# Weights of a mixer stage turned from 64-bit to 32-bit numbers: leading part plus the rest, with an accumulating transfer for the channel weights

## The chip, the cores and the metric

The kernel runs on one NeuronCore of one Trainium2 chip. The metric is the device time of one execution in microseconds (us). The kernel before takes 478.04 us, the median of 3 runs (477.49 to 479.05).

The engines that matter are TensorE (PE in the profile; its weight loads are listed apart as PEld), VectorE (DVE), ScalarE (ACT), GpSimd (POOL) and SyncE (SP), which here only issues transfers. An engine takes its own instructions strictly in the order in which they stand in its program and waits on semaphores for the others.

## The reference

Two stages follow each other for each of 4 batches. The first is a linear attention with a decaying state (8 heads of 48, 768 tokens):

```python
for t in range(S):
    cur = einsum('bhd,bhe->bhde', u[None] * kt, vt)
    y[:, :, t] = einsum('bhd,bhde->bhe', rt, state + cur)
    state = wt[:, :, :, None] * state + einsum('bhd,bhe->bhde', kt, vt)
```

Its output, as x of 768 tokens by 384 channels per batch, goes through a mixer over tokens and then one over channels:

```python
h  = maximum(x.T @ w_tok1, 0) @ w_tok2        # 768 -> 256 -> 768, over tokens
u  = x + h.T
h2 = maximum(u @ w_ch1, 0) @ w_ch2            # 384 -> 1536 -> 384, over channels
out = u + h2
```

The four weights are made as float32 numbers times a numpy scalar of 64 bits, and come to the kernel as 64-bit floating point. [...]

## The kernel before, in words

**Attention.** Each batch is cut into 3 units of 256 tokens. For one unit, DVE runs two scans over the decays (`ends` L456, `begins` L464) and scales keys and queries (L461, L467). PE makes the products inside chunks of 64 tokens (`grams` L336), the state updates (`outer` L386, `update` L529) and the outputs (`across` L401, `within` L422). ACT scales the state from chunk to chunk (`scaled` L522), copies the results out of PSUM (`taken` L428), and reads the range of the decays into flags (`ranges` L448). In batch 0 the state goes around a ring: ACT scales it (L522), PE adds the next chunk to it (L529), ACT scales the sum, twelve chunks long.

**Mixer.** In batch 0, PE runs `hidden` (L968), `back` (L979), a transposition (`turn` L990), `up` (L1014) and `down` (L1025) with float32 weights; ACT rectifies (L971, L1017) and copies the transposed rows (L992), DVE adds into x (L981). From batch 1 on, PE uses split forms of the weights, which ACT and DVE make from the converted ones (`splits`, L600 to L622).

**Conversion.** `conversion` cuts the weights into steps of 128 partitions by 1024 numbers: 3 steps for the two token weights, 9 for the two channel weights (steps 0 to 8 here; w_ch1 fills steps 0 to 3 and half of step 4, w_ch2 the rest). Before, a step is two loads of 512 KB (L280), then: DVE masks the exponent out of the top 16 bits (`exponent` L283) and the mantissa out of the high word (`mantissa` L289) and adds the low word times 2^-32 to it (`add` L295); ACT makes a power of two from the exponent (`raise_two` L286) and a sign from the high word (`signs` L292); DVE multiplies the two (`signed` L298), and multiplies the mantissa by that (`put` L305, in two instructions where a step spans two weights or a piece doesn't lie in one pattern).

**What sets the order.** The list in the call of `strict` at L1116 to L1131 fixes the order of every engine up to the first `back`, by hand. It holds the three steps of the token weights and step 0 of the channel weights. From there on, the digits of `ORDER` say which of nine streams gives the next piece, and `weights_in_turn` (L1196) is the stream of the channel steps, each laid out by `single` (L1137). In `single` the tuples with a queue and a duration are costs for the planner that once made `ORDER`; they set no time when the kernel runs. Each engine keeps that order exactly. Loads of a step go out on SP's queue, two steps ahead, and wait until the raw words of the step that used the room before are read. POOL has no work of the conversion; its first product (L786) comes far behind it.

**Who needs a step.** PE's `up` for the hidden blocks 0 to 3 needs steps 0 and 1, blocks 4 to 7 steps 1 and 2, blocks 8 to 11 steps 3 and 4. PE does `up` for two segments of 256 tokens in turn: the first four matmuls of block 0 need step 0 alone, the fifth needs step 1. `down` follows, in pairs of blocks, twice each, over steps 4 to 8.

Of the kernel before, what the change touches and what calls it, by code (L numbers as in the profile page):

```python
# [10 lines left out]
f32 = mybir.dt.float32  # L11
# [4 lines left out]
u16 = mybir.dt.uint16  # L16
u32 = mybir.dt.uint32
# [47 lines left out]
def rwkv6_then_mixer(  # L65
# [8 lines left out]
    w_tok1: bass.AP,  # L74
    w_tok2: bass.AP,
    w_ch1: bass.AP,
    w_ch2: bass.AP,
# [157 lines left out]
    wtok2 = wts.tile([128, DTOK // 128, S], f32, name="wtok2")  # L235
    now = {"wch1": wts.tile([128, DM // 128, DCH], f32, name="wch1"), "wch2": wts.tile([128, NJ, DM], f32, name="wch2"),
           "wtok1": wtok1, "wtok2": wtok2}

    def conversion_tiles(name):
        t = wide.tile([128, 12 * PIECE], u32, name=name, tag="raw")  # L240
        return t[:, :7 * PIECE], t[:, ds(7 * PIECE, 4 * PIECE)], t[:, ds(11 * PIECE, PIECE)]

    scratch, spare, powers = conversion_tiles("raw")
# [3 lines left out]
    def conversion_rooms(scratch, spare, powers):  # L247
        return ([t[:, :4 * PIECE] for t in (scratch, spare, early[0])], [scratch[:, ts(2, 2 * PIECE)], early[1][:, :2 * PIECE]],
                [[t.bitcast(u16) for t in (scratch[:, ts(6, PIECE)], powers)], [early[1][:, ts(n, PIECE)].bitcast(u16) for n in (2, 3, 4)]])

    bits64, mantissas, exponents = conversion_rooms(scratch, spare, powers)

    def convert(pair, raw, room, signs_at=None):

        d64 = bits64[raw]
        lo, hi = (d64.rearrange("p (n two) -> p n two", two=2)[:, :, j] for j in range(2))
        top = d64.bitcast(u16).rearrange("p (n four) -> p n four", four=4)[:, :, 3]
        m, planes = mantissas[room], exponents[room]
        mf, e, power = m.bitcast(f32), *planes[:2]
        sign, factor = planes[2 * room].bitcast(bf16) if signs_at is None else signs_at, power.bitcast(bf16)  # L260

        (a, _), (b, _) = pair
        c, k = a.shape[1:]
        (row, _), (one, _) = a.ap[1:]
        apart = b.offset - a.offset if a.tensor is b.tensor else None
        beside = apart == k * one
        if beside:
            whole = bass.AP(a.tensor, a.offset, [list(a.ap[0]), [row, c], [one, 2 * k]])
        elif apart is not None and (c == 1 or apart == c * row):
            whole = bass.AP(a.tensor, a.offset, [list(a.ap[0]), [apart // c, 2 * c], [one, k]])  # L270
        else:
            whole = None

        def load():
            for n, (dst, src) in enumerate(pair):
                if beside:
                    to = d64.rearrange("p (c n k) -> p n c k", n=2, c=c)[:, n]
                else:
                    to = d64[:, ts(n, 2 * PIECE)].rearrange("p (c k) -> p c k", c=dst.shape[1])
                sp.dma_start(to, src)  # L280

        def exponent():
            dve.tensor_scalar(e, top, 0x7FF0, None, op0=ALU.bitwise_and)  # L283

        def raise_two():
            act.activation(power, e, AF.Relu, bias=rebias, scale=8.0)  # L286

        def mantissa():
            dve.tensor_scalar(m, hi, 0xFFFFF, 0x100000, op0=ALU.bitwise_and, op1=ALU.bitwise_or)  # L289

        def signs():
            act.activation(sign, hi.bitcast(i32), AF.Sign)  # L292

        def add():
            dve.scalar_tensor_tensor(mf, lo, 2.0 ** -32, m, op0=ALU.mult, op1=ALU.add)  # L295

        def signed(on=dve):
            on.tensor_tensor(factor, factor, sign, ALU.mult)  # L298

        def put(whole_step=True):  # L300
            if whole_step:
                signed()
            for dst, cols in [(whole, slice(0, 2 * PIECE))] if whole is not None else [(dst, ts(n, PIECE)) for n, (dst, _) in enumerate(pair)]:
                x, by = (t[:, cols].rearrange("p (c k) -> p c k", c=dst.shape[1]) for t in (mf, factor))
                dve.scalar_tensor_tensor(dst, x, 2.0 ** -20, by, op0=ALU.mult, op1=ALU.mult)  # L305

        put.apart = lambda on: (lambda: signed(on), lambda: put(False))
        return load, exponent, mantissa, raise_two, add, signs, put

    def blocks(t, src, c, k):  # L310

        bits = src.bitcast(u32).rearrange("(c p) k -> p c k", p=128)
        at = [(i, j) for j in range(0, t.shape[2], k) for i in range(0, t.shape[1], c)]
        return [(t[:, ds(i, c), ds(j, k)], bits[:, ds(i, c), ds(2 * j, 2 * k)]) for i, j in (sorted(at) if c == 4 else at)]

    def conversion(*weights, rooms):
        pieces = [e for w in weights for e in blocks(*w)]
        return [convert(pieces[2 * n:2 * n + 2], *rooms(n)) for n in range(len(pieces) // 2)]
# [992 lines left out]
    with within_range.Else():  # L1311
# [8 lines left out]
        for steps in conversion((now["wtok1"], w_tok1, 2, 256), (now["wtok2"], w_tok2, 2, 256), rooms=lambda n: (n % 2, n % 2)):  # L1320
            for f in steps:
                f()
# [39 lines left out]
```

## Time and profile before

| What | us |
|---|---|
| median of 3 runs | 478.04 (477.49 to 479.05) |
| profiled execution, first to last instruction (span) | 476.6 |
| busy time of PE, PEld, DVE, ACT, POOL in it | 458.4, 409.1, 353.0, 263.8, 54.2 |

The profile has no separate time for the execution that it shows; the median of the runs is 1.4 us above its span, which holds what lies around the first and last instruction and the difference between executions. The profile's page lists busy time by engine, then the span in 40 slices, then the chain of work that ended last, followed back from the end: an engine with a large share there sets the time. Further views of the same trace are used: groups of instructions of one shape, the busy time of each engine in stretches of the span, instructions in order of time with the idle time before them and its releaser in square brackets, the chain in order of time (start, duration, what), and the issues of transfers with their time to landing. PE lists a float32 matmul of `up` as two records.

### The profile page before, as it was taken

The page shows a single profiled execution, that of the slowest core. Times are in us where ns is not written, and L with a number is a line of the kernel's source. Part 1 is how long each engine was busy: PE and PEld are TensorE (multiplying, and loading weights), DVE is VectorE, ACT ScalarE, POOL GpSimd, SP SyncE. Part 2 cuts the span into 40 slices and gives each one's busy share as a digit, 9 for nine tenths or more (in the row PEclk, how much of TensorE's full clock was granted, in tenths as well). Part 3 has the DMA queues.
Part 4 walks back from the last instruction along what each step waited for, and adds up shares of the span by engine and source line. Part 5 has one row for each costly group of instructions (what it writes and reads, how often), then busy time and mean ns, then how long its engine had stood idle before and what let it go on. Part 6 is the DMA issues. An engine that isn't in the chain of part 4 may idle for free.

```text
span 476.6 us, 12802 instructions
## 1 busy us (share of the span) xinstructions
PE 458.4 (96%) x5322; PEld 409.1 (86%) x5322; DVE 353.0 (74%) x506; ACT 263.8 (55%) x606; POOL 54.2 (11%) x58
## 2 busy tenths in 40 slices
PE   3799999999999999999999999999999999999995
PEld 2686688856797668999999999999999999999995
DVE  7999899998598877876897998685587885235331
ACT  6689876773678856353747485251827554134040
POOL 1000000000000001140303002130304003022030
PEclk9979999999999999999999999999999999999999
DMA  8956946753585556853979752754785503437321
GB/s 304 335 170 217 253 146 193 235 221 99 147 232 136 179 189 219 267 182 99 272 275 237 278 158 55 211 168 143 205 230 162 176 30 91 124 86 211 86 86 54
DMA packets 49984, 85.35 MB, mean 179 GB/s; under 512 B 4928, under 2 KB 40640, under 8 KB 49920
## 3 DMA queue, kind: packets, MB, share of 16 engines
q1 hardware_dynamic: 49632, 84.37, 56.9%
q8 instruction: 43, 0.70, 0.6%
q14 instruction: 21, 0.17, 0.1%
q10 hardware_dynamic: 288, 0.10, 0.1%
HBM read 72.65 MB, written 11.80 MB: 177 GB/s over the span
## 4 chain that ended last, share of the span: by engine, by line
PE 92%; DMA 3%; ACT 2%; DVE 1%; SPq 1%; issue 0%; DVEq 0%; ACTq 0%
PE bank L1025 10%; PE bank L793 8%; PE bank L800 8%; PE bank L795 8%; PE bank L811 8%; PE bank L813 8%; PE bank L812 8%; PE bank L1014 7%; PE bank L688 3%; PE bank L747 3%; PE bank L1010 3%; PE bank L336 2%; PE bank L422 2%; PE bank L401 2%; PE kv_ps L386 2%; PE bank L690 2%
## 5 line engine op out<-in xcount | busy, mean ns | idle before, releaser
L786 POOL TENSOR_TENSOR z_high<-z_high 128x384 fp32r<-128x384 f32 x48 | 52.9, 1107 | 406.0 <-DMA ring<-third 186.3
L775 ACT ACTIVATE z_high<-bank 128x384 fp32r<-128x384 f32 x48 | 23.5, 489 | 57.8 <-PE bank L800 57.3
L793 PE MATMUL bank<-x_forms,forms 128*128 128x384 f32 x216 | 50.3, 341 | 0.0
L800 PE MATMUL bank<-z_more,forms 128*128 128x384 f32 x216 | 50.1, 340 | 0.0
L782 DVE SCALAR_TENSOR_TENSOR z_high<-bank,z_high 128x384 fp32r<-128x384 f32 x48 | 26.5, 555 | 30.9 <-ACT z_high L775 30.1
L795 PE MATMUL bank<-x_forms,ring 128*128 128x384 f32 x216 | 49.3, 337 | 0.0
L1025 PE MATMUL bank<-wch,z 128*128 128x384 f32 x144 | 48.1, 488 | 0.0
L811 PE MATMUL bank<-forms,z_high 128*128 128x384 f32 x140 | 47.8, 341 | 0.0
L819 DVE SCALAR_TENSOR_TENSOR x<-bank,x 128x384 f32<-128x384 f32 x35 | 18.8, 553 | 39.0 <-PE bank L813 38.9
L813 PE MATMUL bank<-forms,z_high 128*128 128x384 f32 x140 | 47.1, 337 | 0.0
L812 PE MATMUL bank<-ring,z_high 128*128 128x384 f32 x140 | 47.1, 337 | 0.0
L1025 PEld LDWEIGHTS bank<-wch,z 128*128 128x128 f32 x144 | 26.8, 190 | 17.2
L522 ACT ACTIVATE before<-state,to_end 112x48 f32<-112x48 f32 x132 | 33.2, 324 | 11.8 <-DVE state L537 7.6
L800 PEld LDWEIGHTS bank<-z_more,forms 128*128 128x128 f32 x216 | 39.0, 188 | 0.1
L793 PEld LDWEIGHTS bank<-x_forms,forms 128*128 128x128 f32 x216 | 38.3, 188 | 0.5
L795 PEld LDWEIGHTS bank<-x_forms,ring 128*128 128x128 f32 x216 | 38.6, 188 | 0.0
L1014 PE MATMUL bank<-xT,wch 128*128 128x256 f32 x144 | 32.0, 381 | 0.0
L1014 PEld LDWEIGHTS bank<-xT,wch 128*128 128x128 f32 x144 | 27.0, 190 | 3.7
L778 ACT ACTIVATE z_high<-z_high 128x384 fp32r<-128x384 f32 x48 | 25.2, 525 | 3.6
L811 PEld LDWEIGHTS bank<-forms,z_high 128*128 128x128 f32 x140 | 26.3, 188 | 0.2
L812 PEld LDWEIGHTS bank<-ring,z_high 128*128 128x128 f32 x140 | 26.3, 188 | 0.0
L813 PEld LDWEIGHTS bank<-forms,z_high 128*128 128x128 f32 x140 | 26.3, 188 | 0.0
(252 smaller groups left out, 969.2 us busy)
## 6 DMA issues: line engine op xcount, KB each, us to landing
ring<-third SPq DMA_DIRECT2D x144, 192.0 KB, 3.2
raw<-in_w_ch_dram SPq DMA_DIRECT2D x16, 512.0 KB, 4.8
rk<-in_rk_dram SPq DMA_DIRECT2D x36, 192.0 KB, 5.5
near<-in_near_dram SPq DMA_DIRECT2D x8, 768.0 KB, 6.0
w<-in_w_dram SPq DMA_DIRECT2D x10, 520.5 KB, 5.1
vt<-in_v_dram SPq DMA_DIRECT2D x12, 384.0 KB, 5.1
out_dram<-x SPq DMA_DIRECT2D x17, 192.0 KB, 2.5
third<-forms SPq DMA_DIRECT2D x12, 192.0 KB, 4.0
```

What stands on the lines that cost most here:

```text
L522: act.mul(t[:ROWS, a], state[bt, g][:ROWS, a], by_last(c, j)[:, a:a + 1])
L778: act.mul(z_form(jt, 2), z_form(jt, 0).bitcast(f32), 1.0 / BASE)
L782: dve.scalar_tensor_tensor(z_form(jt, 1), a, 0.0, z_form(jt, 0).bitcast(f32), op0=ALU.max, op1=ALU.subtract)
L786: pool.tensor_add(z_form(jt, 2), z_form(jt, 2).bitcast(f32), z_form(jt, 1).bitcast(f32))
L793: pe.matmul(a, up[m], xf(0)[:, m], start=m == 0, stop=False)
L795: pe.matmul(a, low[:, m], xf(1)[:, m], start=False, stop=False)
L800: pe.matmul(banks["a", jt], joint, xf(2)[:, m], start=False, stop=m == 2)
L811: pe.matmul(a, z[0], up, start=first, stop=False, skip_group_check=True)
L812: pe.matmul(a, z[1], held[bt, s, half, 1, jt], start=False, stop=False, skip_group_check=True)
L813: pe.matmul(a, z[2], joint, start=False, stop=last, skip_group_check=True)
L1014: pe.matmul(ps, now["wch1"][:, m, ts(jt, 128)], xT[:, m, ts(s, SEG)], start=(m == 0), stop=(m == DM // 128 - 1))
L1025: pe.matmul(ps, zs[s][:, jt, ts(n, 128)], now["wch2"][:, jt, :], start=(jt == 0), stop=(jt == NJ - 1))
```

## The change

A step's 64-bit number is now taken as a leading part and a rest. The load leaves out the lowest 16 bits, so that the words in SBUF are shifted: the top 16 bits (sign, exponent, 4 bits of mantissa) are one 16-bit integer, and the next 32 bits are one 32-bit word. Eight times the top 16 bits, with the bias moved, are the bits of a bf16 number. ACT writes that for positive numbers (`positive`) and for negative ones (`negative`), both by a rectified linear function, DVE subtracts the two (`lead`), and the result is the leading part with its sign. DVE masks the mantissa away to get the signed power (`raise_two`), multiplies the rest by 2^-36 and the power into the weight's place (`put`), and the leading part is added last. For the token weights DVE does that (`add`); for the channel weights GpSimd issues a transfer from SBUF to SBUF that accumulates in the destination (`add_landing`: bf16 in, added to float32, 1024 numbers on each of 128 partitions; 10 transfers, as step 4 needs two).

The host lays the words out so that a step is one load of 4095 16-bit units on each of 128 partitions in place of two loads with shorter rows. The token weight `wtok2` and the channel weight `wch1` change their layout in SBUF with it, and PE reads them there. PE's order is unchanged.

```diff
+        word = raw_words[raw]
+        rest = word.rearrange("p (n two) -> p n two", two=2)[:, :, 0]
+        top = word.bitcast(i16).rearrange("p (n four) -> p n four", four=4)[:, :, 2]
+        plus, minus = parts[room]
+        leading, power = plus.bitcast(bf16), minus.bitcast(bf16)
         def load():
...
-                sp.dma_start(to, src)
-        def exponent():
-            dve.tensor_scalar(e, top, 0x7FF0, None, op0=ALU.bitwise_and)
-        def raise_two():
-            act.activation(power, e, AF.Relu, bias=rebias, scale=8.0)
-        def mantissa():
-            dve.tensor_scalar(m, hi, 0xFFFFF, 0x100000, op0=ALU.bitwise_and, op1=ALU.bitwise_or)
-        def signs():
-            act.activation(sign, hi.bitcast(i32), AF.Sign)
+            sp.dma_start(word.bitcast(u16)[:, :words.shape[1]], words)
+        def positive():
+            act.activation(plus, top, AF.Relu, bias=rebias, scale=8.0)
+        def negative():
+            act.activation(minus, top, AF.Relu, bias=rebias, scale=-8.0)
+        def lead():
+            dve.tensor_sub(plus, plus, minus)
+        def raise_two():
+            dve.tensor_scalar(minus.bitcast(u16), plus.bitcast(u16), 0xFF80, None, op0=ALU.bitwise_and)
+        def put():
+            for dst, cols in to:
+                dve.scalar_tensor_tensor(dst, rest[:, cols], 2.0 ** -36, power[:, cols], op0=ALU.mult, op1=ALU.mult)
         def add():
-            dve.scalar_tensor_tensor(mf, lo, 2.0 ** -32, m, op0=ALU.mult, op1=ALU.add)
-        def signed(on=dve):
-            on.tensor_tensor(factor, factor, sign, ALU.mult)
-        def put(whole_step=True):
...
-                dve.scalar_tensor_tensor(dst, x, 2.0 ** -20, by, op0=ALU.mult, op1=ALU.mult)
+            for dst, cols in to:
+                dve.tensor_add(dst, dst, leading[:, cols])
+        def add_landing():
+            for dst, cols in to:
+                pool.dma_start(out=dst, in_=leading[:, cols], accum_op=ALU.add)
...
+            steps.append(convert(to, words.bitcast(u16)[n, :, 1:], *rooms(n)))
...
+    for name, of in (("words_tok", (rows("w_tok1"), grouped(rows("w_tok2"), 256))), ("words_ch", (grouped(rows("w_ch1"), PIECE), rows("w_ch2")))):
...
-        whole = [("load", load, ("Q", 5.0, last(2, "add", "signs"))), ("signs", signs, ("ACT", 1.15, k("load") + last(2, "put"))),
-                 ("exponent", exponent, ("DVE", 0.69, k("load") + last(1, "two"))), ("two", raise_two, ("ACT", 1.15, k("exponent") + last(1, "put"))),
-                 ("mantissa", mantissa, ("DVE", 0.69, k("load") + last(1, "put"))), ("add", add, ("DVE", 1.23, k("mantissa"))),
-                 ("put", put, ("DVE", 2.06, k("two", "add", "signs")))]
+        whole = [("load", load, ("Q", 5.0, last(2, "value", "minus"))), ("plus", positive, ("ACT", 1.15, k("load") + last(2, "put"))),
+                 ("minus", negative, ("ACT", 1.15, k("load") + last(2, "value"))), ("lead", lead, ("DVE", 0.69, k("plus", "minus"))),
+                 ("two", raise_two, ("DVE", 0.35, k("lead"))), ("value", put, ("DVE", 1.23, k("two"))), ("put", add, ("Q", 4.0, k("value")))]
```

`ORDER` is unchanged. A channel step still has seven pieces, so a digit of the stream of weights now stands for another piece than before; the list in the call of `strict` is written out anew for the token steps and step 0. Three places matter below. In the rows that follow, line numbers of the kernel before are 17 to 28 above those of the changed one.

On ACT, around the end of `hidden` (the h rows are the rectified sums), the kernel before has

```order
L292 ACTIVATE raw<-xT 128x1024
L292 ACTIVATE z_130<-z_129 128x1024
L971 ACTIVATE h_145<-h_ps 128x384 x2
L286 ACTIVATE z_130<-z_130,rebias 128x1024
L448 ACTIVATE junk,flags<-first,most 112x1041
L448 ACTIVATE junk,flags<-to_end_93,most 112x1041
L292 ACTIVATE first<-raw 128x1024
L286 ACTIVATE raw<-raw,rebias 128x1024
```

and the changed kernel has

```order
L264 ACTIVATE z_130<-z_129,rebias 128x1024
L267 ACTIVATE z_130<-z_129,rebias 128x1024
L954 ACTIVATE h_145<-h_ps 128x384 x2
L431 ACTIVATE junk,flags<-to_end_93,least 112x1041
L431 ACTIVATE junk,flags<-first,most 112x1041
L431 ACTIVATE junk,flags<-to_end_93,most 112x1041
L264 ACTIVATE raw<-raw,rebias 128x1024
L267 ACTIVATE raw<-raw,rebias 128x1024
```

The last two rows of each are step 1 of the channel weights. Between h and them stand one step of the conversion and two readings of ranges before, and three readings of ranges now; the third one stood further ahead.

On DVE, the same place (the x rows are `back`'s sums). Before:

```order
L298 TENSOR_TENSOR z_130<-z_130 128x1024
L305 SCALAR_TENSOR_TENSOR wch_126<-z_130 128x2x512
L283 TENSOR_SCALAR raw<-raw 128x1024
L981 TENSOR_TENSOR x<-x,bank_881 128x384
L981 TENSOR_TENSOR x<-x,bank_882 128x384
L289 TENSOR_SCALAR raw<-raw 128x1024
L295 SCALAR_TENSOR_TENSOR raw<-raw 128x1024
L981 TENSOR_TENSOR x<-x,bank_884 128x384
L298 TENSOR_TENSOR raw<-raw,first 128x1024
L305 SCALAR_TENSOR_TENSOR wch_126<-raw 128x2x512
```

and now:

```order
L277 SCALAR_TENSOR_TENSOR wch_126<-z_129,z_130 128x1024
L964 TENSOR_TENSOR x<-x,kv_ps 128x384
L964 TENSOR_TENSOR x<-x,bank_873 128x384
L964 TENSOR_TENSOR x<-x,bank_874 128x384
L270 TENSOR_TENSOR raw<-raw 128x1024
L273 TENSOR_SCALAR raw<-raw 128x1024
L277 SCALAR_TENSOR_TENSOR wch_126<-raw 128x1024
L964 TENSOR_TENSOR x<-x,bank_876 128x384
```

Step 0 ends on DVE ahead of `back`'s sums now, and step 1 (`lead`, `raise_two`, `put`) is three rows in place of five. Behind each L277 row, GpSimd issues the accumulating transfer of that step.

On ACT again, further on, among the rectified blocks of `up` (z rows), with what each row waits for, where steps 6, 7 and 8 of the channel weights stand. Before:

```order
L286 ACTIVATE raw<-raw,rebias 128x1024 [waits DVE_49]
L1017 ACTIVATE z_129<-bank_886 128x256 [waits PE_49]
L292 ACTIVATE first<-raw 128x1024 [waits DMAHW6_49,DMAHW5_49,Activation_49]
L1017 ACTIVATE z_130<-bank_881 128x256 [waits PE_49]
L1017 ACTIVATE z_129<-bank_884 128x256 [waits PE_49]
L286 ACTIVATE raw<-raw,rebias 128x1024 [waits DVE_49]
L448 ACTIVATE junk,flags<-to_end_93,most 112x1041 [waits Activation_49]
L292 ACTIVATE first<-raw 128x1024 [waits DMAHW7_49,DMAHW0_49,Activation_49]
```

and now:

```order
L267 ACTIVATE raw<-raw,rebias 128x1024
L1000 ACTIVATE z_130<-bank_874 128x256 [waits PE_49]
L1000 ACTIVATE z_129<-bank_878 128x256 [waits PE_49]
L264 ACTIVATE raw<-raw,rebias 128x1024 [waits DMAHW3_49,DMASW6_49,DVE_49]
L1000 ACTIVATE z_130<-bank_873 128x256 [waits PE_49]
L1000 ACTIVATE z_129<-bank_876 128x256 [waits PE_49]
L267 ACTIVATE raw<-raw,rebias 128x1024 [waits DVE_49]
L431 ACTIVATE junk,flags<-to_end_93,most 112x1041 [waits Activation_49]
L264 ACTIVATE raw<-raw,rebias 128x1024 [waits DMAHW4_49,DMASW7_49,DVE_49]
```

The first row of each is the second ACT instruction of step 6; now it stands one rectified block earlier than before. The last row is the first ACT instruction of step 8. Now it is `positive`, which writes the plane from which step 6's accumulating transfer reads, and so it waits for that transfer (DMASW7). In the same way the first split (L583), which writes into the room of the planes, now waits for the transfers of steps 7 and 8, where it waited for DVE.

143 lines of the change are left out of this document (61 added, 82 removed).

## The prediction

> **What bounds the kernel now.** I read the page first, for the engines and the chain that ended last.
>
> ```profile
> span 476.6 us, 12802 instructions
> PE 458.4 (96%) x5322; PEld 409.1 (86%) x5322; DVE 353.0 (74%) x506; ACT 263.8 (55%) x606; POOL 54.2 (11%) x58
> ...
> PE 92%; DMA 3%; ACT 2%; DVE 1%; SPq 1%; issue 0%; DVEq 0%; ACTq 0%
> ```
>
> PE is busy for 96% of the span and makes up 92% of the chain; DVE, which the change relieves, makes up 1%. Then the stretches of the span (from:to, length, busy time of PE, PEld, DVE, ACT, POOL, granted clock, share of the transfer engines, GB/s), to see where PE has holes:
>
> ```profile
> 12.00:24.00 12.00, 8.93 (x254) 7.26 (x254) 11.79 (x11) 7.44 (x22) 0.00 (x0) 0.91 0.93 331
> ...
> 36.00:48.00 12.00, 11.87 (x281) 7.93 (x280) 11.30 (x14) 11.07 (x27) 0.00 (x0) 1.00 0.62 220
> ...
> 60.00:72.00 12.00, 12.00 (x62) 10.61 (x61) 11.79 (x15) 8.78 (x18) 0.00 (x0) 1.00 0.40 131
> ...
> 84.00:96.00 12.00, 12.00 (x173) 9.87 (x172) 11.80 (x16) 8.51 (x14) 0.00 (x0) 1.00 0.84 254
> ```
>
> The holes are in the start. From 60 to 96 us DVE is nearly as full as PE, but PE has no hole there that a lighter DVE could close. The chain in order of time (start, duration, what) shows what stands on the path:
>
> ```profile
> 14.32 6.32 DMA first<-in_rk_dram
> ...
> 44.70 4.88 PE h_ps L968 x14
> ...
> 58.84 11.66 PE bank L1014 x54
> ...
> 73.67 17.03 PE bank L1014 x78
> ...
> 94.00 15.48 PE bank L1025 x48
> ```
>
> From 44.70 on PE runs through `hidden`, `back`, `up` and `down` back to back. A microsecond that PE waits here is one at the end; one that DVE saves here is worth nothing unless PE had waited for it.
>
> **What the change takes away and adds, by engine.** The groups of the first 135 us by shape (count, busy, mean ns of one, idle before):
>
> ```profile
> L295 DVE SCALAR_TENSOR_TENSOR raw<-raw 128x1024 f32<-128x1024 uint32 x9 | 11.0, 1223 | 0.2
> L305 DVE SCALAR_TENSOR_TENSOR wch<-raw 128x1024 f32<-128x1024 f32 x6 | 7.3, 1225 | 0.2
> ...
> L289 DVE TENSOR_SCALAR raw<-raw 128x1024 uint32<-128x1024 uint32 x9 | 6.2, 686 | 0.0
> L283 DVE TENSOR_SCALAR raw<-raw 128x1024 uint16<-128x1024 uint16 x9 | 6.1, 677 | 0.0
> ...
> L298 DVE TENSOR_TENSOR raw<-raw,first 128x1024 bf16<-128x1024 bf16 x8 | 5.5, 685 | 0.1
> ```
>
> A step cost DVE 0.68 + 0.69 + 1.22 + 0.69 + 1.23 = 4.5 us. Now `lead` is nearest to L298 (two 16-bit planes, 0.69) and `put` to L295 (1.22). The mask over a dense 16-bit plane has no row; L283 reads every fourth and takes 0.68, so it lies between 0 and 0.68, and I take 0.4. That is 2.3 us for a channel step and 3.5 with the token steps' `add` (1.22 more). DVE is spared 9 x 2.2 + 3 x 1.0 = 23 us, and none of it is on the path. ACT has two instructions of 1.15 us per step as before:
>
> ```profile
> L286 ACT ACTIVATE raw<-raw,rebias 128x1024 uint16<-128x1024 uint16 x10 | 11.5, 1148 | 6.0 <-DVE raw L283 5.9
> L292 ACT ACTIVATE first<-raw 128x1024 bf16<-128x1024 int32 x8 | 9.3, 1157 | 0.3 <-ACT junk L448 0.3
> ```
>
> The 5.9 us in which ACT waited for `exponent` go; what is late next behind them is PE's bank, as ACT's z rows wait for PE.
>
> **The start, up to 44 us.** PE goes step by step with ACT around the state's ring, and ACT has as many instructions in it as before, at the same places. ACT itself stands still once:
>
> ```profile
> 20.75 0.91 ACT L352 ACTIVATE near<-first,u_col 112x256 f32<-112x256 f32 x2 [3.12 <-DMA first<-in_rk_dram]
> ```
>
> That load is queued behind the raw words of the first token step, which now come in one transfer of longer rows that start 2 bytes off. The issue of a second load goes (SP), its bytes stay. No row has such a transfer; a gain of 0.3 or a loss of as much is my estimate from the 6.32 us that the row of the chain gives for the pair of loads, and I take 0. On DVE the token steps' rows move, so the masks must be looked at; the last one, of unit 2, is the tightest:
>
> ```profile
> 37.20 1.16 ACT L286 ACTIVATE z<-z,rebias 128x1024 uint16<-128x1024 uint16 x1
> ...
> 40.93 1.32 DVE L348 COPY_PREDICATED at<-before_it,gram 128x1024 f32<-128x1024 uint8 x1 [0.16 <-PE gram L336]
> ...
> 43.55 1.15 PE L422 MATMUL y_ps<-vt,at 64*64 64x48 f32 x64
> ```
>
> Token step 1's second part takes the place of the ACT row and ends at 38.3; `lead`, the mask of bits, and `put` and `add` in halves (0.6 + 0.4 + 2.4) end at 41.7, and the mask at 43.1, 0.45 ahead of the PE row that needs it. So the start stays.
>
> **The first term: step 1, at 60 us.** PE enters `up` at 58.84. The first four matmuls (8 records at 17.03 / 78 = 0.218 us) need step 0, so step 1 is needed at 60.6. Before, it was ready at 59.25 (last row):
>
> ```profile
> 49.61 0.49 ACT L971 ACTIVATE h<-h_ps 128x384 f32<-128x384 f32 x1 [0.80 <-PE h_ps L968]
> 50.00 1.14 ACT L286 ACTIVATE z<-z,rebias 128x1024 uint16<-128x1024 uint16 x1
> 51.04 1.15 ACT L448 ACTIVATE junk<-first,most 112x1041 uint8<-112x1041 f32 x1
> ...
> 53.48 1.14 ACT L292 ACTIVATE first<-raw 128x1024 bf16<-128x1024 int32 x1
> 54.52 1.14 ACT L286 ACTIVATE raw<-raw,rebias 128x1024 uint16<-128x1024 uint16 x1
> ...
> 58.02 1.23 DVE L305 SCALAR_TENSOR_TENSOR wch<-raw 128x1024 f32<-128x1024 f32 x1
> ```
>
> Now ACT reads three ranges after h, each (53.48 - 51.04) / 2 = 1.22, from 50.00 to 53.7, then makes step 1's two parts, 1.04 each from start to start, to 55.7. DVE follows with 0.7 + 0.4 + 1.22, to 58.1. There the conversion ended before; now an accumulating transfer begins. With X for the time from the end of `put` to the landing, PE waits 58.1 + X - 60.6 = **X - 2.5**.
>
> **X has no row.** GpSimd issues no transfer before. The nearest are SP's (bytes each, median us from issue to landing):
>
> ```profile
> raw<-in_w_ch_dram SPq DMA_DIRECT2D x16, 512.0 KB, 4.8
> ...
> near<-in_near_dram SPq DMA_DIRECT2D x8, 768.0 KB, 6.0
> ...
> out_dram<-x SPq DMA_DIRECT2D x17, 192.0 KB, 2.5
> ...
> z_more<-kept SPq DMA_DIRECT2D x2, 384.0 KB, 7.7
> ```
>
> A step's transfer writes 512 KB and reads 256 of the leading part and 512 of the destination, 768 in all. By what it writes it is nearest to the first row, by what it reads to the second; I take the middle, X = 5.4. Ends: 2.5 (192 KB, an idle queue) and 7.7 (384 KB among others). So the first term is 2.9, from 0 to 5.2.
>
> The Trainium skill ("DMA: Bandwidth & Descriptors", section "Anatomy of one DMA — SWDGE (gpsimd) path") puts a transfer issued by GpSimd at about 2.0 us plus its bytes by 436 GB/s, 3.2 us for 512 KB; by that estimate the first term would be 0.7. No run here shows such a transfer yet.
>
> Step 0 ends on DVE near 50.7, two rows later than ACT's parts at 48.4, and has 8.1 us until 58.84. Step 2 ends near 61.5 and is needed 9 us after step 1. Step 4 follows ACT's z rows at 74 and is needed at 82. These have room for X.
>
> **The second term: steps 6 to 8, at 85 to 105 us.** Here a wait is added: `positive` of a step waits for the transfer of two steps earlier, and with it, on ACT's queue, the z rows behind.
>
> ```profile
> 85.56 0.39 ACT L1017 ACTIVATE z<-bank 128x256 f32<-128x256 f32 x1 [0.89 <-PE bank L1014]
> ...
> 99.21 3.78 ACT L600 ACTIVATE forms<-wch 128x768 fp32r<-128x768 f32 x5 [1.60 <-DVE wch L305]
> ...
> 113.48 0.84 ACT L622 ACTIVATE forms<-forms 128x768 fp32r<-128x768 f32 x1 [2.77 <-DVE starts L452]
> ...
> 120.88 0.86 ACT L371 COPY kT<-bank 128x384 f32<-128x384 f32 x2 [3.74 <-PE bank L366]
> ```
>
> `negative` of step 6 follows the z row of 85.56 and ends at 87.0. DVE has `lead`, the mask, the scaling of the queries (1.1, it stands between) and `put`: 90.3. The transfer lands at 90.3 + X, and only then `positive` of step 8 starts. Two on ACT (2.1) and 0.7 + 0.4 + 0.3 (a state copy) + 1.22 on DVE give 95.0 + X, and its transfer lands at 95.0 + 2X. PE needs step 8 with block 9 of `down`: 17 matmuls of 15.48 / 24 = 0.645 behind 94.00, at 105.0. PE waits 2X - 10.0: **0.8** at 5.4, 5.4 at 7.7, nothing up to 5.0. Both sides are moved by the first term alike.
>
> The splits (L600) then start at 105.8 in place of 99.2, 6.6 us late. The idle time of 2.77 and 3.74 us in the two last rows takes most of it, and PE first reads a split form at 130 us, so I cost it at nothing; without that cover it would be up to 6.6. POOL's ten transfers come long before its first product, and cost nothing there. SP's loads of steps 3 to 8 wait for `put` where they waited for `add`, which is up to 2 us later for step 8 (90.3 against 88.2); `positive` of that step waits for a transfer beyond it anyway.
>
> **Sum.** 2.9 + 0.8 = 3.7 on a span of 476.6, which gives 480.3. The profile has no time beside its span; the median lies 1.4 above it. With the same 1.4: **481.7 us**.
>
> **The rivals.** First, *the transfer lands early* (not slower). If X is at most 3.9, the first term is at most 1.4, the second is 0, and the kernel stays within 0.3%, which is 1.4 us and about what a measurement here can tell from no change. At the row of 2.5 us it gives 478.0, at 3.2 us 478.7. For it: the transfer stays inside SBUF, and the share of the transfer engines in 60 to 72 us is 0.40. Against it: the row of 512 KB takes 4.8, and this one reads its destination too. It decides at X = 3.9. The skill's fit above speaks for it. Chance 0.26.
>
> Second, *the transfers crowd* (slower still). In 84 to 96 us the share is 0.84, before ten transfers are added. At X = 7.7 the terms are 5.2 and 5.4: 488.6. For it: the row of 384 KB with 7.7. Chance 0.2 for X above 6.4, which is where the sum passes 6.7.
>
> Third, *the start gets shorter* (faster). If the longer rows bring the load of the chain's first row early by more than the first term and 1.4 us, the kernel is faster. The row of 512 KB at 4.8 against 6.32 leaves at most 1.5 us, so X must be under 2.6 at the same time. Chance 0.05. That the change doesn't do what it says can be left out of the time: DVE's work goes in any case, and nothing on the path is bought with it.
>
> A further cost could come with the first: the Trainium skill ("TensorE: Matmul & The Clock Gate", section "HAM oscillation — how this bites in real kernels") warns of gaps of PE over about 3.4 us, after which its clock is halved for a while. The stretch of 12 to 24 us, with PE's holes, has a granted clock of 0.91, which agrees in kind. It is not in the sum.
>
> **How the numbers follow.** My forecast, X from 3.9 to 6.4, has 0.49, and gives 479.4 to 484.7; with the first rival 0.26, the second 0.2, the third 0.05. The range of 8 in 10 takes in the first rival down to its row of 2.5 us with the estimate of 0.3 for the load, and the second up to X = 7.3 (4.8 + 4.6): 477.9 to 487.4. Slower by over 0.3%: 0.49 + 0.2 = 0.69 and a share of the first rival's edge, 0.70; faster 0.05; within, 0.25.
>
> **What would show it right or wrong.** In the profile of the changed kernel: PE with a wait at its second pair of matmuls in `up`, near 60 us, for a transfer into the channel weight, of about 2.9 us; DVE's busy time lower by about 23 us with no gain; ACT with a wait ahead of `positive` of step 8; PE with a second, shorter wait near block 9 of `down`. It is wrong if PE has no wait there (X under 2.5), if DVE's relief shortens the start, or if PE's time grows without waits.

## The result, and the profile after

The changed kernel takes 500.75 us in the median of 6 runs (494.09 to 507.77), against 477.94 us for the kernel before in the same session (6 runs, 477.21 to 480.87): 1.0388 times as long, 95% interval 1.0351 to 1.0425. The prediction was 481.7 us with a range up to 487.4. The three runs more than 1.5% above the fastest are left out of the ratio but not of the median, so the two don't match. The profiled execution is the fastest of the six, 494.09 us, so the account below is that of 15.8 us of span (492.4 against 476.6), and not of the 22.8 us between the medians.

The page of the changed kernel, with busy times and the shares of the chain:

```profile
span 492.4 us, 12800 instructions
PE 463.5 (94%) x5322; PEld 411.7 (84%) x5322; DVE 333.9 (68%) x485; ACT 265.8 (54%) x606; POOL 63.4 (13%) x68
...
PE 80%; issue 6%; DVE 5%; ACT 4%; DMA 3%; POOL 1%; SPq 0%; DVEq 0%; ACTq 0%; POOLq 0%
```

DVE has 19.1 us less to do, and the kernel is slower all the same. PE fell from 92% to 80% of the chain. The stretches (columns as in the prediction) say where:

```profile
60.00:72.00 12.00, 7.91 (x36) 6.52 (x37) 8.02 (x12) 6.26 (x13) 1.76 (x2) 1.00 0.82 264
...
96.00:108.00 12.00, 9.80 (x156) 6.60 (x155) 3.61 (x5) 4.42 (x7) 1.03 (x2) 1.00 0.81 248
108.00:120.00 12.00, 6.87 (x16) 3.71 (x15) 2.52 (x4) 3.20 (x7) 1.59 (x2) 0.72 0.74 247
```

Two places: 60 to 72 us, and 96 to 120. PE's own instructions in order of time, with the wait ahead of each in brackets, size them:

```profile
44.55 1.24 PE L951 MATMUL h_ps<-x,wtok 128*128 128x384 f32 x3
...
61.00 1.97 PE L997 MATMUL bank<-xT,wch 128*128 128x256 f32 x8 [0.54 <-ACT xT L975]
66.52 10.20 PE L997 MATMUL bank<-xT,wch 128*128 128x256 f32 x46 [3.55 <-DMA wch<-raw]
...
79.81 17.10 PE L997 MATMUL bank<-xT,wch 128*128 128x256 f32 x78
...
100.05 5.32 PE L1008 MATMUL bank<-wch,z 128*128 128x384 f32 x16
107.58 2.85 PE L1008 MATMUL bank<-wch,z 128*128 128x384 f32 x8 [2.20 <-DMA wch<-raw]
115.56 9.88 PE L1008 MATMUL bank<-wch,z 128*128 128x384 f32 x24 [5.13 <-DMA wch<-raw]
125.28 0.82 PE L973 MATMUL bank<-ident,x 128*128 128x128 f32 x6
...
146.65 13.28 PE L993 MATMUL bank<-x_forms,forms 128*128 128x256 f32 x108
```

The same places in the kernel before:

```profile
58.67 11.82 PE L1014 MATMUL bank<-xT,wch 128*128 128x256 f32 x54
...
73.60 17.10 PE L1014 MATMUL bank<-xT,wch 128*128 128x256 f32 x78
...
93.84 15.64 PE L1025 MATMUL bank<-wch,z 128*128 128x384 f32 x48
109.32 0.82 PE L990 MATMUL bank<-ident,x 128*128 128x128 f32 x6
```

`hidden` begins at 44.55 (44.63 before), so the start is unchanged. `up` begins at 61.00 in place of 58.67, 2.3 us late. The fifth matmul (each is two records) then waits 3.55 us, until 66.52. The long run of `up` begins at 79.81 in place of 73.60, 6.2 late: that is the first place. In `down` two waits of 2.20 and 5.13 us stand for transfers, and the 48 records of its first part, 15.64 us before, take 5.32 + 2.85 + 9.88 = 18.05, which is 2.4 more. Together 9.7, and 125.28 is 16.0 us behind the 109.32 of before: that is the second place. The rest of the span adds nothing (15.8 at the end).

The 2.3 us are not all the transfers': 0.82 is a hole inside `hidden` that no releaser explains, 0.6 a wait for ACT ahead of the last transposition, which the kernel without these transfers (the first experiment) has too, and 0.7 stand right ahead of `up`. They are no loss beside the other wait either: PE goes on at 66.52, when step 1 has landed, however early `up` begins.

Why the transfers are late shows in the rows of GpSimd (start and duration of the instruction that issues a transfer):

```profile
51.27 1.03 POOL L285 DMA_DIRECT2D wch<-z  x1 [49.30 <-DVE wch L277]
61.17 0.89 POOL L285 DMA_DIRECT2D wch<-raw  x1 [8.87 <-DVE x L964]
66.73 0.87 POOL L285 DMA_DIRECT2D wch<-raw  x1 [4.67 <-DVE starts L440]
...
97.68 0.88 POOL L285 DMA_DIRECT2D wch<-raw  x1 [5.61 <-DVE wch L277]
107.85 0.87 POOL L285 DMA_DIRECT2D wch<-raw  x1 [9.29 <-issue]
115.83 0.88 POOL L285 DMA_DIRECT2D wch<-raw  x1 [7.11 <-issue]
```

against the ends of `put` on DVE, of steps 0, 1, 6 and 8:

```profile
49.72 1.23 DVE L277 SCALAR_TENSOR_TENSOR wch<-z,z 128x1024 f32<-128x1024 uint32 x1
...
58.11 1.23 DVE L277 SCALAR_TENSOR_TENSOR wch<-raw 128x1024 f32<-128x1024 uint32 x1
...
96.05 1.22 DVE L277 SCALAR_TENSOR_TENSOR wch<-raw 128x1024 f32<-128x1024 uint32 x1
...
111.29 1.22 DVE L277 SCALAR_TENSOR_TENSOR wch<-raw 128x1024 f32<-128x1024 uint32 x1
```

Step 0's transfer begins 0.3 us behind its `put` and its landing, 9.6 us, puts it at 60.9; `up` begins at 61.0. (The view names ACT there, but ACT's copy of chunk 3, that ends then, isn't needed for the first matmuls: in the first experiment `up` begins at 58.47 and that copy at 58.67. It is a releaser that came last by chance.) Step 1's `put` ends at 59.34, but GpSimd begins its transfer at 61.17, when step 0's has landed. Step 1's lands at 66.5 and PE goes on at 66.52; step 2's begins at 66.73. The same again at the end: step 6's is issued at 97.68 and lands at 107.6, step 7's begins at 107.85 and PE goes on at 115.56 when it has landed, step 8's begins at 115.83. The transfers go one at a time. The view names other releasers or "issue" for these waits, as it has no event for them.

The issues of transfers (KB each, median us to landing), and in 48 to 124 us the queues' own rows (packets, MB, share of 16 engines):

```profile
wch<-raw POOLq DMA_DIRECT2D x7, 512.0 KB, 5.9
```

```profile
q1 hardware_dynamic: 2489, 12.18, 49.3%
q0 software_dynamic: 1440, 4.72, 25.3%
```

Nine steps take 25.3% of 76 us of the engines, 2.1 us each if nothing else ran; the median is 5.9 and step 6's 9.9. Here is SP's queue beside step 6's transfer:

```profile
97.72 0.42 SPq L181 DMA_DIRECT2D w<-in_w_dram  x1
98.19 0.43 SPq L201 DMA_DIRECT2D vt<-in_v_dram  x1
98.67 1.44 SPq L1183 DMA_DIRECT2D kept<-wtok  x2
100.15 0.67 SPq L206 DMA_DIRECT2D near<-in_near_dram  x1
```

These are 3.2 MB, and step 8's raw words, 1 MB, are issued at 97.3, when step 6's `put` lets them go: 4.2 MB begin with the transfer. Two theories remain to be told apart, and a third that the rows would also allow. A: the ring, which is the room where GpSimd writes the descriptors of its transfers (512 bytes here), holds one accumulating transfer. B: a transfer is slow because it shares the engines with what SP issues. C: DVE's use of SBUF holds GpSimd back, since its late starts follow runs of DVE.

### The profile page after: what moved, and what is told of

It is laid out like the page before. It is cut to its first block, busy times and chain, and to the rows that moved or that the text cites. A ratio compares the mean times of both kernels' runs of the same rounds, so it can differ in the third digit from the quotient of the medians.

```text
span 492.4 us, 12800 instructions
## 1 busy us (share of the span) xinstructions
PE 463.5 (94%) x5322; PEld 411.7 (84%) x5322; DVE 333.9 (68%) x485; ACT 265.8 (54%) x606; POOL 63.4 (13%) x68
## 4 chain that ended last, share of the span: by engine, by line
PE 80%; issue 6%; DVE 5%; ACT 4%; DMA 3%; POOL 1%; SPq 0%; DVEq 0%; ACTq 0%; POOLq 0%
PE bank L776 8%; PE bank L783 8%; PE bank L778 8%; PE bank L794 8%; PE bank L796 7%; PE bank L795 7%; PE bank L1008 4%; PE bank L997 3%; PE bank L671 3%; PE bank L993 3%; PE bank L730 3%; PE bank L405 2%; DMA wch<-raw 2%; PE bank L319 2%; PE bank L384 2%
## 5 line engine op out<-in xcount | busy, mean ns | idle before, releaser
L1008 PE MATMUL bank<-wch,z 128*128 128x384 f32 x144 | 50.5, 504 | 7.3 <-DMA wch<-raw 7.3
L270 DVE TENSOR_TENSOR raw<-raw 128x1024 int16<-128x1024 int16 x11 | 7.6, 691 | 31.0 <-ACT raw L267 31.0
L794 PEld LDWEIGHTS bank<-forms,z_high 128*128 128x128 f32 x140 | 26.3, 188 | 0.2
```

Source lines behind the costliest of these rows:

```text
L794: pe.matmul(a, z[0], up, start=first, stop=False, skip_group_check=True)
L1008: pe.matmul(ps, zs[s][:, jt, ts(n, 128)], now["wch2"][:, jt, :], start=(jt == 0), stop=(jt == NJ - 1))
```

## Experiments

**DVE adds the leading part in all steps.**

```diff
-rooms=lambda n: (n % 2, n % 2, True) if n else (2, 2, True))
+rooms=lambda n: (n % 2, n % 2, False) if n else (2, 2, False))
```

> The accumulating transfers of the channel weights are replaced by DVE's add (nine steps, ten instructions of 1.2 us or less); everything else of the change stays. If the transfers are the whole cause, step 1 is ready at 59.34 + 1.2 = 60.5 for a need at 62.97 and the splits start near 99 us again: 477 to 479 us. Rival, that the new loads or the new order of ACT's rows cost time themselves: 483 us or more.

478.17 us (10 runs), 1.0015 times before, interval 1.0002 to 1.0027. Its PE has no wait at either place, but for 0.60 us at 58.12 ahead of the last transposition:

```profile
58.47 11.82 PE L997 MATMUL bank<-xT,wch 128*128 128x256 f32 x54
...
93.64 15.64 PE L1008 MATMUL bank<-wch,z 128*128 128x384 f32 x48
```

So the transfers are the whole loss, to within the 0.3% of the interval. The new loads and conversion, which spare DVE 8.4 us here (344.6 against 353.0), give nothing and cost nothing that matters: DVE's time had been no bound.

**Room for more transfers, with a control.** The kernel gets more room for descriptors. To make space for them, the rooms of the decayed states go from five to four, first alone.

```diff
-name="before", bufs=5
+name="before", bufs=4
-dynamic_dma_scratch_size=512
+dynamic_dma_scratch_size=1024
```

> A control for the next two: the changed kernel with four instead of five rooms for the decayed states (768 bytes per partition less), nothing else. All theories: as the changed kernel, 494 to 502 us. If it is slower by over 1%, the next two are read against it.

> As the control, with 1024 in place of 512 bytes for the descriptors of GpSimd's transfers. Theory A, the ring has room for one transfer, and GpSimd begins the next when the one before has landed: GpSimd now starts at most 0.5 us behind the put of steps 1 and 2 (1.8 and 3.7 in the changed kernel), step 7's start no longer waits 5.3 us for step 6's landing, and the time is 482 to 489 us. Theory B, the transfers share the engines with SP's loads: GpSimd starts early, but the landings take as much longer, 492 to 500 us. Theory C, DVE's use of SBUF holds GpSimd's descriptors up: the starts stay at 1.8 and 3.7 us, and so does the time, 494 to 502 us.

> 2048 bytes for the descriptors, four rooms for the decayed states and two for the states. Theory A: no start of GpSimd is late any more, 480 to 487 us, as with 1024 bytes or a little less. Theories B and C: as the control, 492 to 502 us.

The control takes 499.32 us (1.0446, 1.0373 to 1.0519), as the changed kernel. With 1024 bytes it is 495.55 (1.0389, 1.0349 to 1.0428), with 2048 bytes (and two rooms in place of three for the states) 496.71 (1.0395, 1.0356 to 1.0434). GpSimd and PE with 1024:

```profile
58.61 0.86 POOL L285 DMA_DIRECT2D wch<-raw  x1 [6.26 <-DVE wch L277]
62.31 0.86 POOL L285 DMA_DIRECT2D wch<-raw  x1 [2.83 <-DVE starts L435]
...
106.08 0.87 POOL L285 DMA_DIRECT2D wch<-raw  x1 [5.54 <-DVE wch L277]
```

```profile
67.36 11.88 PE L997 MATMUL bank<-xT,wch 128*128 128x256 f32 x46 [3.96 <-DMA wch<-raw]
```

Every step's transfer now starts 0.3 to 0.4 us behind its `put`, with the same work on DVE beside it: A is right about the starts, C is out. The Trainium skill ("SBUF — State Buffer", section "Who interferes with whom") warns that DVE can keep GpSimd from writing descriptors; this trace doesn't show it, as GpSimd's instruction takes 0.86 us at 62.31, where DVE scans, and at 91.94, where DVE stands still. But PE goes on at 67.36, where it was 66.52 in the changed kernel's profile and 71.17 in the control's, whose execution took 501.56 us: the median landing rose from 7.1 us in the control's profile to 8.8. A's gain to 482 to 489 us didn't come, and both times lie in B's 492 to 500; the intervals of the three overlap, so a gain of a few us is neither shown nor excluded. Two transfers that share the engines seem to land about when the second of two in turn would have.

**The two places apart, then both.**

```diff
-rooms=lambda n: (n % 2, n % 2, True) if n else (2, 2, True))
+rooms=lambda n: (n % 2, n % 2, n > 1) if n else (2, 2, n > 1))
```

for the first, `n < 6` for the second, `1 < n < 6` for both.

> DVE adds the leading part of steps 0 and 1, transfers add that of steps 2 to 8. If the two places are apart and add up, this takes away the late start of up (2.3 us in the changed kernel's profile) and the wait of 3.55 us for step 1, and leaves what steps 6 to 8 cost (9.7 us): 486 to 491 us. Rival, that the transfers crowd each other all along: steps 6 to 8 get cheaper too, below 485 us.

> DVE adds the leading part of steps 6, 7 and 8, transfers add that of steps 0 to 5. If the two places add up, the waits of PE in down (2.2 and 5.1 us, and 2.4 us of slower clock behind them) go and the 6 us of step 1 and the start of up stay: 482 to 486 us. The splits start behind DVE's add of step 8 again, so if it was their late start that set the time, it goes too, with the same number; if the splits were late for another reason, 490 us or more.

> DVE adds the leading part of steps 0, 1, 6, 7 and 8; transfers add only that of steps 2 to 5, the ones that the prediction gave room. If they have room, PE doesn't wait for them and the time is that of DVE's add in all steps, 477 to 480 us. If each transfer takes 8 us and they come one behind the other, PE waits for them in up (1.25 and 0.98 us with steps 0 and 1 alone on DVE) and the time is 481 to 486 us.

Steps 0 and 1 on DVE: 493.73 us (1.0331, 1.0268 to 1.0394), above the 486 to 491 expected. `up` began at 58.20 without a wait, but PE then waited 1.25 us at 70.4 and 0.98 at 84.5 for later steps, and 0.72 and 5.95 in `down`. A PE that isn't late meets the same queue of transfers a step further on. Another 2.58 us at 96.4 were for DVE's scaling of the queries: `lead` of step 6 stands ahead of it on DVE, and ACT's `positive` for that had waited 5.42 us for a transfer. Steps 6 to 8 on DVE: 488.57 (1.0250, 1.0172 to 1.0328), also above its 482 to 486: the waits in `down` are gone, and so are the late splits, but in this profile the first place costs 10.6 us (the first product of `down` at 104.41 against 93.84), as step 0 took 10.3 us and step 1 8.6; some 3.6 of it is a halved clock behind the waits (3.41 us for the eight records and 12.35 for the 46, in place of 1.97 and 10.20). The two places do not simply add up, and the landings differ from execution to execution. Both on DVE: 481.10 (1.0058, 1.0027 to 1.0088), the low edge of the case without room; its profile, 479.13 us, has one wait for a transfer, of 0.68 us for step 2's.

**The transfer without adding.**

```diff
-pool.dma_start(out=dst, in_=leading[:, cols], accum_op=ALU.add)
+pool.dma_start(out=dst, in_=leading[:, cols])
```

> GpSimd's transfers write the leading part over the destination in place of adding it, so the weights lack their rest. If it is the reading and adding at the destination that makes a transfer take 5 to 10 us, landings fall to 3 to 4 us and the time to 480 to 486 us. If the time goes to the queue of transfers and to SP's loads beside them, the landings stay within 1.5 us of those before and the time at 490 to 502 us.

The weights of this kernel lack their rest; only its time counts. 489.46 us (1.0249, 1.0189 to 1.0309), between the two cases and just under the 490 of the second, while the landings fit the second: median 6.4, longest 10.1. In 48 to 124 us its queue takes

```profile
q0 software_dynamic: 1440, 4.72, 19.7%
```

which is 1.7 us of the engines for a step in place of 2.1. And GpSimd starts step 1 at 59.20, before step 0 has landed, with the same 512 bytes. So adding costs 0.5 us of engine time a step and the room for a second transfer, but it isn't what makes 10 us out of 2.

**Neighbours taken away, one after the other.** First the stores of the token weights wait for step 8; then, apart from that, the loads of steps 3 to 8 are left out; then both, with the load of unit 4's decays behind step 6.

```diff
-lambda i=i: sp.dma_start(kept[i], wtok1...
+behind("landed", lambda i=i: sp.dma_start(kept[i], wtok1...
```

(`"landed"` names the last accumulating transfer built by then, here that of step 8; for the load of the decays it is step 6's.)

```diff
-each[n].insert(-1, each[n + 2].pop(0))
+name, load, ops = each[n + 2].pop(0)
+each[n].insert(-1, (name, lambda: None, ops))
```

```diff
-piece(lambda: load_w(i + 1), "w",
+piece(behind("landed", lambda: load_w(i + 1)) if i == UB else lambda: load_w(i + 1), "w",
```

> As the changed kernel, but the two stores of the token weights (768 KB each), and with them the load of near behind them on SP's queue, wait until step 8's transfer has landed. In the changed kernel step 6's transfer, issued at 97.7, takes 9.9 us beside them. Theory B, transfers share the engines with what SP issues: step 6 lands within 6 us, PE's two waits in down shrink from 7.3 to under 3 us, 485 to 490 us. Rival, an accumulating transfer of this size takes 8 to 10 us by itself: PE's waits and the time stay, 492 to 502 us.

> As the changed kernel, but the loads of the raw words of steps 3 to 8 are left out (those steps convert old words, so the weights are others). The put of a step releases both its own transfer and the load of the step two behind it, 1 MB; here the transfers have no such neighbour. Theory B, they are slow because of that neighbour: the landings of steps 1 to 5 fall to 3.5 to 5 us, GpSimd's starts come early with them, and the time to 480 to 488 us. Rival, that transfers hold each other up and are slow alone: landings of 7 us and more, 492 to 502 us.

> The loads of raw words of steps 3 to 8 are left out (so the weights are others), the load of the decays of unit 4 waits until step 6's transfer has landed, and the two stores of the token weights, with near behind them, until step 8's has. If step 6's neighbours are the cause at the second place, it lands within 5 us, PE's waits in down fall from 5.9 (2.83, 1.39 and 1.64 with the raw loads alone left out) to under 1.5 us, and the time from 493.4 to 484 to 489 us. If transfers of these steps are slow without neighbours, 491 to 495 us.

Without the stores: 495.75 us (1.0385, 1.0305 to 1.0465). Step 6 still took 9.2 us, beside step 8's load, `w` and `vt`; only step 7's, 7.7 us before, fell to 4. The 485 to 490 of theory B failed, and the time lies in its rival's 492 to 502; but step 7's 4 us speak against a transfer that is slow by itself, and 1.9 MB beside step 6 had stayed, the load of 1 MB among them that its own `put` releases. Without the loads of steps 3 to 8 (these steps convert old words, so the weights are others): 493.41 (1.0313, 1.0268 to 1.0359), also outside B's 480 to 488 and inside its rival's, but the landings are B's:

```profile
51.20 1.03 POOL L285 DMA_DIRECT2D wch<-z  x1 [49.22 <-DVE wch L277]
62.07 0.89 POOL L285 DMA_DIRECT2D wch<-raw  x1 [9.85 <-DVE raw L273]
...
96.70 0.88 POOL L285 DMA_DIRECT2D wch<-raw  x1 [6.79 <-DVE wch L277]
108.05 0.87 POOL L285 DMA_DIRECT2D wch<-raw  x1 [10.47 <-issue]
...
DMA to landing us min/median/max: 3.0/3.9/11.0
```

The median is 3.9 where a transfer is alone, and two remain slow: step 0's beside eight loads of `rk`, step 6's with 11.0 beside the burst, here at 95 to 98 us. These two set the time. With both kinds of neighbour taken away from step 6: 487.80 us (1.0213, 1.0159 to 1.0266), as expected; it landed within 4.9 us (step 7 starts at 100.58, behind a start at 95.72), and the second place shrank to 1.59 + 0.77 us.

**And room for two, and step 0 on DVE.** The last kernel with the edits of the control and of 1024 bytes, and then with this as well:

```diff
-rooms=lambda n: (n % 2, n % 2, True) if n else (2, 2, True))
+rooms=lambda n: (n % 2, n % 2, n > 0) if n else (2, 2, n > 0))
```

> The same, with 1024 bytes for the descriptors and four rooms for the decayed states, so that step 1's transfer begins beside step 0's. If neighbours and the room for one transfer are the whole cause, step 1 lands by 65 us, PE waits under 2 us for it, and the time is 478 to 483 us. If something else makes up late at 60 us, 484 us or more.

> As the run before it (loads of raw words of steps 3 to 8 left out, other loads and stores moved behind transfers, 1024 bytes for descriptors), with step 0's leading part added by DVE; steps 1 to 8 still go by transfers. If step 0's transfer is what is left, up begins by 59.5 us and the time is 478 to 482 us. If ACT's queue holds PE's up back, up begins after 61 us and the time stays at 484 to 487 us.

With 1024 bytes besides: 485.75 us (1.0164, 1.0124 to 1.0204), 3 above its range and in the case where something else makes `up` late. No wait for step 1 is left and 0.31 us in `down`; what is left is this:

```profile
51.82 1.02 POOL L285 DMA_DIRECT2D wch<-z  x1 [49.85 <-DVE wch L277]
```

```profile
62.30 11.98 PE L998 MATMUL bank<-xT,wch 128*128 128x256 f32 x54 [2.39 <-ACT near L336]
```

Step 0's landing of 10.4 us puts it at 62.2, and `up` begins at 62.30. With that step on DVE, 483.73 (1.0110, 1.0080 to 1.0140), between the two cases. There `up` begins right behind the last transposition, with no wait ahead of it, which speaks for step 0's transfer; but at 61.28, since the start is late in this profile (`hidden` at 45.31, and a hole of 1.05 us in it with no releaser). Step 1 costs 1.57 us more and step 7's place 0.52. The loads around step 0's transfer were never taken away; that they make it slow is argued from the other steps. That it is the first transfer of the program isn't the reason: here step 1's is the first, with no load beside it, and takes 4.0 us. So the room for one transfer, the neighbours of the later steps and step 0's transfer hold most of the loss: of 3.9% by the ratio 1.1% is left, some 5 us, of which 2.1 are still waits for transfers and some 3 are not settled.

**The best of them.** DVE's add, and the reading of a range back ahead of `lead` of the last token step.

```diff
-rectified[1], e1["ranges"][0], e2["ranges"][1],
+rectified[1], e2["ranges"][1],
-e2["seen"], n2, e2["after"], lead2,
+e2["seen"], n2, e2["after"], e1["ranges"][0], lead2,
```

> DVE adds the leading part in all nine channel steps, and the reading of a range that the change had moved behind h stands further ahead on ACT again. In the kernel with DVE's add, PE waited 0.60 us at its last transposition for ACT's second part of step 1, which stands behind that reading: this goes, 0.3 to 0.8 us less than 478.2, so 477.4 to 477.9 us, a ratio to the kernel before of 0.998 to 1.001. Rival, that PE has other work late by as much: no change, 478.2 us.

477.83 us (12 runs), 0.9976 times before, interval 0.9946 to 1.0006. The wait of 0.60 us at the transposition is gone, as expected (the ACT row that ended it had been step 2's second part, not step 1's), but no gain over the kernel before is shown, nor over DVE's add alone, whose interval overlaps it.

## Why the prediction was wrong

**What bounds the kernel, and DVE's relief: right.** DVE lost 19.1 us of busy time (23 forecast; summed row by row, where neighbours overlap, it lost some 22), and neither the changed kernel nor the one with DVE's add gained from it. The rows behind it:

```profile
L277 DVE SCALAR_TENSOR_TENSOR wch<-raw 128x1024 f32<-128x1024 uint32 x7 | 8.6, 1223 | 0.2
...
L270 DVE TENSOR_TENSOR raw<-raw 128x1024 int16<-128x1024 int16 x11 | 7.6, 691 | 31.0 <-ACT raw L267 31.0
L273 DVE TENSOR_SCALAR raw<-raw 128x1024 uint16<-128x1024 uint16 x11 | 4.7, 427 | 0.4
```

1.22, 0.69 and 0.43 us, where the prediction took 1.22, 0.69 and 0.4.

**The start up to 44 us: right**, 44.55 for 44.63.

**"X has no row ... I take the middle, X = 5.4": this step failed.** From the end of `put`, X was 9.9 for step 0, 7.1 for step 1, 10.3 for step 6. It was taken once for all steps, from medians of SP's transfers over the whole program, where the engines are mostly less full (a share of 0.93 in 48 to 60 us of before, 0.53 behind 200 us). The rows for the right size were in the profile of before: eight loads of `rk` (192 KB each) and the raw words of two steps are issued from 41.9 to 53.3 us there, as from 41.8 to 54.3 in the changed kernel, and in 40 to 62 us of before

```profile
rk<-in_rk_dram SPq DMA_DIRECT2D x8, 192.0 KB, 9.3
```

so even 192 KB took 9.3 us there. In that neighbourhood step 0's transfer took 9.6. A transfer alone took 3.9 us (no loads of raw words), so the bound of 2.5 was too low as well, and 7.7 was no upper bound.

**"Step 0 ... has 8.1 us until 58.84": the room was rightly sized and too small** for 9.9. What it cost stood in no term: 0.7 us right ahead of `up`, and, which decides, 1.8 us by which step 1's transfer begins late behind it.

**The first term, 58.1 + X − 60.6: right in form.** `put` ended at 59.34, 1.2 later than worked out, 0.8 of it by the hole in `hidden`; with an earlier `put` X would have been as much longer, as step 0 landed no earlier for it. With the measured 7.1 it gives 5.8, and PE lost 2.3 + 3.6 = 5.9. Of the 7.1, 1.8 is the wait until step 0 had landed.

**The second term, 2X − 10.0: the wrong link.** ACT did wait for step 6's transfer ahead of `positive` of step 8, as forecast, and the splits waited for step 8's:

```profile
107.61 1.22 ACT L264 ACTIVATE raw<-raw,rebias 128x1024 int16<-128x1024 int16 x1 [6.38 <-DMA wch<-raw]
...
120.18 3.78 ACT L583 ACTIVATE forms<-wch 128x768 fp32r<-128x768 f32 x5 [7.76 <-DMA wch<-raw]
```

But PE didn't wait for step 8. It waited for step 6 itself, and then for step 7, whose transfer GpSimd couldn't begin for 5.3 us. For these two the prediction had worked out no time of need; at its own 0.645 us a matmul they are needed 8 and 12 matmuls behind 94.00, at 99.2 and 101.7, well ahead of step 8's 105.0. The prediction also listed what is queued behind the new wait on ACT, and passed over GpSimd's queue with "cost nothing there": it asked what comes late on that engine, not whether one transfer holds up the next. This term was 0.8 and came to 9.7.

**The splits, costed at nothing: not refuted.** They began 21 us late, and PE reached the first split product 16.85 us late with 16.0 lost before: 0.9 at most, which the end doesn't show.

**The clock, left out of the sum.** In the wait of 5.13 us the granted clock (the column ahead of the last two) fell, and behind it it was halved:

```profile
111.00:114.00 3.00, 0.00 (x0) 0.00 (x0) 1.50 (x3) 1.01 (x4) 0.00 (x0) 0.76 1.07 352
114.00:117.00 3.00, 1.44 (x2) 0.84 (x3) 0.00 (x0) 0.00 (x0) 0.88 (x1) 0.50 0.14 36
```

and 24 records took 9.88 us in place of 7.8. That is 2.1 of the 2.4 us by which the first part of `down` is longer.

**The rivals.** The second, crowding, is what happened, with one transfer at a time on top; it had a chance of 0.2 and its price by one row of 7.7 us, so that even it ended at 488.6. It argued from the share of 84 to 96 us; the two places that count lie before and behind. The first rival had the fit of the Trainium skill ("DMA: Bandwidth & Descriptors", section "Anatomy of one DMA — SWDGE (gpsimd) path") on its side, by which such a transfer takes an estimated 3.2 us; one that is alone took 3.9 us here, but neither of the two that set the time was alone. The third is out, as the start didn't get shorter. The lower end of the range should have been 478.0 - 0.3 = 477.7 by its own words, not 477.9; nothing hangs on that.

The spread of the runs, 494 to 508 us, isn't explained by one profile. The control, profiled at 501.56 us, has a median landing of 7.1 us against 5.6, which points to the transfers, and a halved clock behind its waits at the first place (eight records in 3.75 us and 46 in 12.08, in place of 1.97 and 10.20). It wasn't tried further.

## What to carry to other kernels

Price an added transfer at its place, not by a median: list what the queues hold in the microseconds around its issue (here 4.2 MB at one place), and ask which load the same instruction releases. Ask of an engine that issues several whether the second can start before the first has landed, and follow the steps one behind the other. Work taken from an engine that bounds nothing buys nothing, so anything late on the new way is a loss.

## What the runs showed of the hardware

With 512 bytes for descriptors, accumulating transfers of 128 rows went strictly one at a time; plain ones of the same size did not, and with 1024 bytes neither did accumulating ones. The late starts fell from 1.8, 3.7 and 5.3 us to 0.3 to 0.4.

A transfer of 512 KB took 3.9 us alone and 9 to 11 beside a few MB of loads, with 2.1 us of the engines' own time.

PE's clock didn't go by the length of one gap. In the changed kernel a wait of 3.55 us left it at 1.00 and 46 records took 10.20 us. In the kernel without the loads of steps 3 to 8, a stretch with waits of 0.61 and 1.71 us (PE busy for 0.7 us of the three from 59 to 62) was followed by eight records of 3.57 us, where 1.97 is usual:

```profile
61.90 3.57 PE L997 MATMUL bank<-xT,wch 128*128 128x256 f32 x8 [1.71 <-issue]
```

The Trainium skill ("TensorE: Matmul & The Clock Gate", section "HAM oscillation — how this bites in real kernels"), which the prediction cited for gaps over about 3.4 us, agrees for the waits of 5.13 and 3.96 us, and not for these two.

A hole of 0.3 to 1.2 us inside `hidden`, near 46 us, with no releaser, shows in some profiles (0.82 in the changed kernel) and not in others. Its cause is open.
